# Source order for TensorE, ScalarE and VectorE in a gated mix of linear attention and a squared-ReLU MLP

## The chip, the cores and the metric

The kernel runs on one core of a Trainium2 chip. A core has engines that run side by side, each with an instruction queue of its own: TensorE (PE in the profile, matmuls into PSUM banks; PEld are its weight loads), VectorE (DVE), ScalarE (ACT), GpSimd (POOL) and SyncE (SP, which here only starts DMAs). They wait for each other by semaphores. The metric is the device time of one execution in microseconds (us).

## What is computed

For x of 2048 tokens by 448, with 16 heads of 28 and a hidden width of 1792:

```python
qkv = (x @ wqkv) ...            # q, k, v: 16 heads of 28
phi = lambda t: jnp.where(t > 0, t + 1, jnp.exp(t)) + 1e-6
pq, pk = phi(q), phi(k)
kv = jnp.einsum("bhsd,bhse->bhde", pk, v)
z = jnp.einsum("bhsd->bhd", pk)
num = jnp.einsum("bhqd,bhde->bhqe", pq, kv)
den = jnp.einsum("bhqd,bhd->bhq", pq, z)[..., None] + 1e-6
a = (num / den) ... @ wo
h = jnp.einsum("bsd,df->bsf", x, w1) + b1
r = jnp.where(h > zero, h, zero)
b = jnp.einsum("bsf,fd->bsd", r * r, w2) + b2
g = _sigmoid((x * gate_w).sum(-1, keepdims=True))
return g * a + (1 - g) * b
```

Everything is float32.

## The kernel before

Every float32 operand of a matmul is split into a high part (rounded to the matmul's own type, the name ends in h) and a low part (the rest, the name ends in l), and a product is made as high by high, high by low and low by high. The high part is a copy with a conversion, mostly on ACT (`split_hi`, line 58) and for the hidden values on DVE (line 62); the low part is a subtraction on DVE, for `nl` on POOL (`split_lo`, line 65).

The tokens are four blocks of 512, each of four tiles of 128. The hidden width is 14 chunks f of 128. `up(b, f)` makes the hidden chunk in `h_ps` (line 214: 11 matmuls of 512 columns, since the last of four chunks c of the 448 inputs needs two terms only), `hidden` takes ReLU and square on ACT (lines 222, 223, tile `hr`) and splits on DVE (`hh`, `hl`), and `down(b, f)` adds the chunk to the four output tiles `o_ps` (line 245: 12 matmuls of 448 columns). An up is always one chunk ahead of its down.

Pass 1 goes over blocks 0 to 3 with f 0 to 6. It also makes, tile by tile, the keys (`k_ps`, 11 matmuls of 448 columns, `phi` into `r`, split into `ph` and `pl`), the gate's logits, and per block the gram of keys and tokens (`g_ps`, 11 or 8 matmuls for each of four c, out of the `ph`, `pl` and the split tokens `nh`, `nl` of all four tiles). Then key sums and the product with v are made. Pass 2 goes over blocks 3, 0, 1, 2 with f 7 to 13, each with queries (`q_ps`, c = 3 first; `swap` brings the last query chunk's partitions into order with eight DMAs `qr<-qv`, `join` adds both), the sum `ds` of queries times key sums, its split `dh`, `dl`, the matmul `d_ps` that spreads it over a head, `rec` (1e-6 added, four reciprocals), the scaled queries (`qh`, `ql`) and, tile by tile, `attention` (`a_ps`, 11 matmuls, then `u` on ACT and `part` on DVE). In the first of these blocks the matrix `m_s` is made out of `wo` and the gram: four m products, each split and then moved by five DMAs on POOL's queue. `finish` adds the gated parts and stores a tile.

PSUM has eight banks: four for `o_ps` (pool `acc_p`), two for `h_ps` (`mm_p`), two for everything else (`ms_p`, taken in turn by the scheduler's count). SBUF buffers for short-lived tiles come from 15 slots.

The source gives the steps in a rough order, with the parts that follow a matmul put off by `run_todo`. The order on every engine is decided by a scheduler: it interleaves the matmuls of one step with those of another and picks, on ACT and DVE, what its own plan has ready first. One place is tied by hand, with `tc.issue_after`, which keeps `d_ps` behind the last down (line 454).

At the start, 18 matmuls on zeros keep PE at work (line 164) while x and w1 come in by chunks c, w1 before x, the first x in two halves; the first four hidden chunks are made together, chunk c by chunk c (lines 501 to 512).

Of the kernel before, what the change touches and what calls it, by code (L numbers as in the profile page):

```python
# [30 lines left out]
def gated_mix_kernel(ctx: ExitStack, tc: tile.TileContext, xt, xn, wk, wq, wv, wo, w1a, w1b, w2, b1, b2, gw, hmask,  # L31
# [125 lines left out]

    warm = keep.tile([P, 400], mybir.dt.bfloat16, name="warm")[:, :256]  # L160
    dve.memset(warm, 0.0)
    warm_ps = acc_p.tile([P, 512], F, name="warm_ps", tag="acc")
    for _ in range(18):
        pe.matmul(warm_ps[:, :256], warm[:, :P], warm, start=True, stop=True)
# [39 lines left out]
    def up_chunk(ps, b, f, c):  # L204
# [8 lines left out]
        for n, (a, m) in enumerate(terms):  # L213
            pe.matmul(ps, a, m, start=(c == 0 and n == 0), stop=(c == 3 and n == 1))  # L214
# [546 lines left out]
```

## Time and profile before

| | |
|---|---|
| time, median of 3 runs (lowest, highest) | 441.72 us (441.72, 441.75) |
| the profiled execution, and its span | 441.68 us, 439.9 us |
| granted TensorE clock, mean | 0.998 |
| busy: PE, DVE, ACT, POOL | 431.6, 281.4, 172.2, 63.0 us |
| first matmul of the computation, start of the last | 5.28 us, 435.57 us |

A row of the timeline gives the start in us from the span's start, the duration, the engine, the line, the operation with output and inputs by the program's names, the shape and how many instructions are grouped; in brackets the idle time just before it and what ended it. A row of the waits gives the waiting engine with its output, what it waited for, the total, the number of times and the longest. A row of the issues of DMAs ends with the count, the size and the median us from issue to landing.

### The profile page before, as it was taken

The numbers are of one execution on the slowest core, as the hardware profiler recorded it, in microseconds if no ns is written. First come the engines' busy times: TensorE is split into PE (matmuls) and PEld (weight loads), VectorE is DVE, ScalarE is ACT, GpSimd is POOL, SyncE is SP. The second block draws the span as 40 slices with busy tenths as digits, with TensorE's granted clock in tenths as the row PEclk, the third lists the DMA queues.
The fourth block names the chain that finished last, engine by engine and source line by source line (L and its number), as shares of the span: only waits on it lengthen the run. The fifth ranks groups of instructions, "written<-read, shape, count | busy, mean of one in ns | idle before, by whom it ended". The sixth has DMA issues, their size and how long they took to land.

```text
span 439.9 us, 5510 instructions
## 1 busy us (share of the span) xinstructions
PE 431.6 (98%) x2054; PEld 380.5 (86%) x2054; DVE 281.4 (64%) x470; ACT 172.2 (39%) x300; POOL 63.0 (14%) x76
## 2 busy tenths in 40 slices
PE   8999899999999999999999989999999999999996
PEld 6898798899898889898988868889888898888895
DVE  5969538662689428792466678788455984549423
ACT  5955235331346113542344335345332453234321
POOL 0144124210244005420002420000000000000000
PEclk9999999999999999999999999999999999999999
DMA  8852302021031210332146311040100501002002
GB/s 268 224 155 58 99 0 66 28 66 47 24 115 34 67 45 5 107 102 82 54 125 148 73 38 24 1 154 26 25 0 0 182 0 25 0 1 85 0 1 83
DMA packets 18459, 29.00 MB, mean 66 GB/s; under 512 B 2896, under 2 KB 12928, under 8 KB 18432
## 3 DMA queue, kind: packets, MB, share of 16 engines
q1 hardware_dynamic: 17216, 27.04, 20.3%
q0 software_dynamic: 1216, 1.61, 1.9%
q8 instruction: 16, 0.26, 0.3%
q14 instruction: 11, 0.09, 0.1%
HBM read 22.31 MB, written 3.67 MB: 59 GB/s over the span
## 4 chain that ended last, share of the span: by engine, by line
PE 90%; DVE 4%; ACT 1%; issue 1%; DMA 1%; SPq 1%; DVEq 0%; ACTq 0%
PE o_ps L245 29%; PE h_ps L214 28%; PE q_ps L77 8%; PE a_ps L77 8%; PE g_ps L77 8%; PE k_ps L77 7%; DMA xr<-in_xt 1%; PE kv_ps L372 1%; SPq L51 1%; PE m_ps L77 1%; DVE w L65 1%; DVE wk_s L65 0%; ACT hr L222 0%; DVE r L266 0%; PE d_ps L77 0%
## 5 line engine op out<-in xcount | busy, mean ns | idle before, releaser
L214 PE MATMUL h_ps<-xh,w 128*128 128x512 f32 x392 | 126.5, 391 | 0.5 <-ACT xh L58 0.4
L245 PE MATMUL o_ps<-w,hh 128*128 128x448 f32 x448 | 125.5, 363 | 0.4 <-DVE hh L62 0.4
L245 PEld LDWEIGHTS o_ps<-w,hh 128*128 128x128 f32 x448 | 83.9, 188 | 9.7 <-DVE hh L62 1.0
L214 PE MATMUL h_ps<-xl,w 128*128 128x512 f32 x224 | 87.6, 391 | 0.0
L214 PEld LDWEIGHTS h_ps<-xh,w 128*128 128x128 f32 x392 | 73.6, 188 | 15.2 <-ACT xh L58 0.7
L245 PE MATMUL o_ps<-w,hl 128*128 128x448 f32 x224 | 79.9, 364 | 0.0
L222 ACT ACTIVATE hr<-h_ps,b_s 128x512 f32<-128x512 f32 (+1 forms) x57 | 38.4, 675 | 97.3 <-PE h_ps L214 90.2
L62 DVE CAST hh<-hr 128x512 fp32r<-128x512 f32 (+1 forms) x57 | 26.1, 458 | 39.1 <-ACT hr L223 38.9
L214 PEld LDWEIGHTS h_ps<-xl,w 128*128 128x128 f32 x224 | 42.1, 188 | 8.2 <-DVE xl L65 0.5
L245 PEld LDWEIGHTS o_ps<-w,hl 128*128 128x128 f32 x224 | 42.1, 188 | 2.9 <-DVE hl L65 0.2
L65 DVE TENSOR_TENSOR hl<-hr,hh 128x512 fp32r<-128x512 f32 (+1 forms) x57 | 41.2, 722 | 1.9
L223 ACT ACTIVATE hr<-hr 128x512 f32<-128x512 f32 (+1 forms) x57 | 35.3, 622 | 1.3
L77 PE MATMUL k_ps<-wk_s,xh 128*128 128x448 f32 x112 | 33.0, 362 | 0.0
L77 PE MATMUL q_ps<-xh,wq_s 128*128 128x512 f32 x100 | 33.0, 390 | 0.0
L65 POOL TENSOR_TENSOR nl<-xnr,nh 128x384 fp32r<-128x384 f32 x16 | 18.7, 1166 | 95.2 <-ACT nh L58 95.2
L77 PE MATMUL a_ps<-m_s,qh 128*128 128x448 f32 x112 | 32.2, 362 | 0.0
L289 POOL TENSOR_TENSOR ksum<-ksum,r 128x448 f32<-128x448 f32 x15 | 22.8, 1517 | 46.7 <-DVE r L266 41.3
L490 DVE SCALAR_TENSOR_TENSOR part<-part,gate,u 128x448 f32<-128x448 f32 x16 | 10.9, 683 | 24.9 <-ACT u L489 24.9
L489 ACT ACTIVATE u<-a_ps,gate 128x448 f32<-128x448 f32 x16 | 10.1, 634 | 37.2 <-PE a_ps L77 37.2
L77 PE MATMUL g_ps<-ph,nh 128*128 128x448 f32 x64 | 23.2, 363 | 0.7 <-ACT ph L58 0.7
L77 PE MATMUL g_ps<-pl,nh 128*128 128x448 f32 x64 | 23.3, 364 | 0.5 <-DVE pl L65 0.5
L77 PE MATMUL q_ps<-xl,wq_s 128*128 128x512 f32 x60 | 23.4, 390 | 0.0
(105 smaller groups left out, 562.2 us busy)
## 6 DMA issues: line engine op xcount, KB each, us to landing
xr<-in_xt SPq DMA_DIRECT2D x27, 256.0 KB, 2.8
xnr<-in_xn SPq DMA_DIRECT2D x16, 224.0 KB, 2.6
out<-out SPq DMA_DIRECT2D x16, 224.0 KB, 2.0
w2r<-in_w SPq DMA_DIRECT2D x14, 224.0 KB, 2.7
w1r<-in_w1a SPq DMA_DIRECT2D x8, 256.0 KB, 2.7
w1r<-in_w1b SPq DMA_DIRECT2D x8, 192.0 KB, 2.9
m_s<-m POOLq DMA_DIRECT2D x12, 112.0 KB, 2.6
wqr<-in_wq SPq DMA_DIRECT2D x4, 256.0 KB, 3.1
```

Source lines behind the costliest of these rows:

```text
L51: sp.dma_start(out=dst, in_=src)
L62: eng.tensor_copy(hi, src)
L65: eng.tensor_tensor(lo, src, f32(hi), op=ALU.subtract)
L77: pe.matmul(out_ps, a, b, start=(i == 0), stop=(i == n - 1))
L214: pe.matmul(ps, a, m, start=(c == 0 and n == 0), stop=(c == 3 and n == 1))
L222: act.activation(r[:, c], ps[:, c], AF.Relu, bias=b1_s[:, f:f + 1])
L223: act.activation(r[:, c], r[:, c], AF.Square)
L245: last = pe.matmul(o_ps[i][:, :D], a, m, start=(f % NH == 0 and n == 0), stop=(f % NH == NH - 1 and n == 2))
L289: pool.tensor_tensor(ksum, ksum, p, op=ALU.add)
L372: pe.matmul(kv_ps[:JE, js], wv_s[c][:, js], gsum[c][:, js], start=(c == 0), stop=(c == 3))
L489: act.activation(u, ps[:, :D], AF.Copy, scale=gate[:, 0, t:t + 1])
L490: dve.scalar_tensor_tensor(part[t], part[t], gate[:, 1, t:t + 1], u, op0=ALU.mult, op1=ALU.add)
```

## The change

The change has three parts. First, PE, ACT and DVE take their instructions in the order of the source (`tc.manual_schedule`); SP and POOL stay with the scheduler. The source is rewritten to be that order: `run_todo` stands ahead of an up or behind it as the place needs, with `join` steps last; the keys' work is cut into `first` and `rest`; `split_den`, `denominators`, `scaled`, `attention`, the splits of wo and of the kv product, and the m products have places of their own; and the end of the last block takes its last attention behind up 13 and the two last chunks' downs in the order 12 for three tiles, then 13, with the fourth tile last. Second, the start: x is loaded before w1, the first w1 chunk in two halves, the twelve matmuls of the first chunk go term by term over the four hidden chunks, 15 warm-up matmuls stand where 18 did (on zeros that lie in `part[0]`), the second group of w1 is loaded behind wk, and the keys of tile 0 stand ahead of the first down, with their PSUM banks out of `acc_p` and `mm_p`. Third, buffers and small steps: the two other PSUM banks are taken by name in turn (`bank`), the m products use `mm_p`, 1e-6 is added by one ACT copy from PSUM into `rec` in place of two DVE additions of 256 columns, half of the swap's DMAs are issued by POOL, the split kv and wo tiles lie in the late pool, and some weights' tiles change their padding.

The core of the diff:

```diff
+    ms_p = ctx.enter_context(tc.tile_pool(name="ms_p", bufs=1, space=PSUM))
+    turn = [0]
+
+    def bank(name):
+        turn[0] ^= 1
+        return ms_p.tile([P, 512], F, name=name, tag=f"ms{turn[0]}")
 
...
+    ctx.enter_context(tc.manual_schedule(engines={pe.engine, act.engine, dve.engine}))
+
+
+    part = [keep.tile([P, D], F, name=f"part{t}") for t in range(NT)]
+    warm = part[0].bitcast(mybir.dt.bfloat16)[:, :256]
     dve.memset(warm, 0.0)
     warm_ps = acc_p.tile([P, 512], F, name="warm_ps", tag="acc")
-    for _ in range(18):
+    for _ in range(15):
         pe.matmul(warm_ps[:, :256], warm[:, :P], warm, start=True, stop=True)
...
     for c in range(4):
-        load_w1(0, 0, c)
+        load_x(0, c)
         if c == 0:
-            load_x(0, c, 0, TB // 2)
-            load_x(0, c, TB // 2, TB)
-        else:
-            load_x(0, c)
+            load_w1(0, 0, c, 0, TB // 2)
+            load_w1(0, 0, c, TB // 2, TB)
+        else:
+            load_w1(0, 0, c)
...
-        def after():
+        def first():
             phi(ps[:, :D], e, r, p)
+
+        def rest():
+            nh = tmp.tile([P, 512], R, name=f"nh{t}", tag="nh", bufs=4)
+            nl = tmp.tile([P, 384], R, name=f"nl{t}", tag="nl", bufs=4)
+            raw = xn_raw.pop(t)
+            split_hi(act, nh[:, :D], raw)
+            split_lo(pool, nl, raw[:, :384], nh[:, :384])
+            split_lo(pool, nh[:, D:], raw[:, 384:], nh[:, 384:D])
+            dve.scalar_tensor_tensor(e, raw, 1.0, gw_s, op0=ALU.mult, op1=ALU.mult, accum_out=logit[:, t:t + 1])
             split_hi(act, ph, p)
             split_lo(dve, pl, p, ph)
             if t == 0:
                 pool.tensor_copy(ksum, p)
             else:
                 pool.tensor_tensor(ksum, ksum, p, op=ALU.add)
-            nh = tmp.tile([P, 512], R, name=f"nh{t}", tag="nh", bufs=4)
-            nl = tmp.tile([P, 384], R, name=f"nl{t}", tag="nl", bufs=4)
-            raw = xn_raw[t]
-            split_hi(act, nh[:, :D], raw)
-            split_lo(pool, nl, raw[:, :384], nh[:, :384])
-            split_lo(pool, nh[:, D:], raw[:, 384:], nh[:, 384:D])
             pend[t] = (ph, pl, nh, nl)
-            return [logits]
...
             act.copy(v, ps)
-            for p in range(0, P, 16):
-                load(r[p:p + 16], v[p ^ 16:(p ^ 16) + 16])
+            for p in range(0, P, 32):
+                load(r[p:p + 16], v[p + 16:p + 32])
+                pool.dma_start(out=r[p + 16:p + 32], in_=v[p:p + 16])
             return [join]
...
-        ps = ms_p.tile([P, 512], F, name=f"d_ps{b}", tag="ms")
-        with tc.issue_after(last.ins):
-            products(ps, [(hm, den.pop((b, "h"))), (hm, den.pop((b, "l")))])
+    def split_den(b):
+        den[b, "h"], den[b, "l"] = slot([P, TB], R, f"dh{b}"), slot([P, TB], R, f"dl{b}")
+        total = den.pop((b, "s"))
+        split_hi(act, den[b, "h"], total)
+        split_lo(dve, den[b, "l"], total, den[b, "h"])
+
+    def denominators(b):
+        ps = bank(f"d_ps{b}")
+        products(ps, [(hm, den.pop((b, "h"))), (hm, den.pop((b, "l")))])
         den[b, "r"] = rec = slot([P, TB], F, f"rec{b}")
 
+        act.activation(rec, ps, AF.Copy, bias=1e-6)
+
         def part_(i):
-            cs = slice(i * 256, (i + 1) * 256)
-            dve.tensor_scalar_add(rec[:, cs], ps[:, cs], 1e-6)
             for j in range(2 * i, 2 * i + 2):
                 dve.reciprocal(rec[:, j * P:(j + 1) * P], rec[:, j * P:(j + 1) * P])
         return [lambda: part_(0), lambda: part_(1)]
...
     def run_todo():
-        now, todo[:] = list(todo), []
+        now, todo[:] = sorted(todo, key=lambda step: step.__name__ == "join"), []
...
+    first = [mm_p.tile([P, 512], F, name=f"h_ps0_{f}", tag="mm") if f < 2 else bank(f"h_ps0_{f}") for f in range(4)]
     for c in range(4):
         if c == 0:
-            split_x(0, 0, 0, TB // 2)
-            split_w1(0, 0, 0, hi_eng=dve)
-            split_x(0, 0, TB // 2, TB)
-        else:
+            xs[0] = new_x(0)
+            w, raw = new_w1(0, 0), w1_raw.pop((0, 0, 0))
+            xh, xl = [x[:, 0] for x in xs[0]]
+            split_hi(act, xh, x_raw[0, 0])
+            split_hi(dve, w[:, 0, :TB // 2], raw[:, :TB // 2])
+            split_lo(dve, xl, x_raw[0, 0], xh)
+            split_hi(dve, w[:, 0, TB // 2:], raw[:, TB // 2:])
+            split_lo(dve, w[:, 4], raw, w[:, 0])
+        else:
+            split_x(0, c)
             split_w1(0, 0, c)
-            split_x(0, c)
-        for f in range(4):
-            up_chunk(first[f], 0, f, c)
-    hidden(first[0], 0, 0, 2)
-    hidden(first[1], 0, 1)
+        if c == 0:
+            for n in range(3):
+                for f in range(4):
+                    up_chunk(first[f], 0, f, c, n)
+        else:
+            for f in range(4):
+                up_chunk(first[f], 0, f, c)
     split_w2(0)
     split_w2(1)
-    for f in range(2, 4):
-        hidden(first[f], 0, f)
-
-    wk_s = keep.tile([P, 7 * D + 48], R, name="wk_s", tag="wkm", bufs=1)
-    wk_s = wk_s[:, :7 * D].rearrange("p (c n) -> p c n", c=7)
-
-    load_xn(0)
+    wk_s = keep.tile([P, 7, D], R, name="wk_s", tag="wkm", bufs=1)
+    for c in range(4):
+        split_w(wk_s, c, wk_raw[c], act, dve)
+    load(gw_s, gw.partition_broadcast(P))
+    load(b2_s, b2.partition_broadcast(P))
+    hidden(first[0], 0, 0)
+    hidden(first[1], 0, 1)
+    k_first, k_rest = keys(0)
+    down(0, 0)
+    k_first()
+    for c in range(4):
+        split_w1(0, 1, c)
     load_w2(2)
     load_w2(3)
-    for c in range(4):
-        split_w(wk_s, c, wk_raw[c], act, dve)
-    down(0, 0)
...
     load_x(1, 3)
     split_x(1, 1)
     split_w2(6)
-    todo += gram(0, 0)
     split_x(1, 2)
     down(0, 5)
-    run_todo()
-    todo += gram(0, 1)
+    todo += gram(0, 0)
     split_x(1, 3)
 
...
                 if b == 1:
-                    todo += gram(0, 2)
-                    run_todo()
-                    todo += gram(0, 3)
-                    run_todo()
+                    for c in range(1, 4):
+                        todo += gram(0, c)
+                        run_todo()
             else:
...
         for f in range(NF - NH, NF):
             fl = f - NH
             run_todo()
+            if fl == (0 if n else 4) and n != 1:
+                split_den(b)
             up(b, f)
...
+                split_x(then, 2 * fl - 2)
+                split_x(then, 2 * fl - 1)
             if fl:
                 if n + 1 < NB or f + 1 < NF:
-                    last = down(b, f - 1)
+                    down(b, f - 1)
             elif n == 0:
                 down(b, NH - 1)
                 half_done(b)
             else:
-                last = down(order[n - 1], NF - 1)
+                down(order[n - 1], NF - 1)
                 for i in range(4):
+                    if n == 1:
+                        attention(order[0], i)
                     finish(order[n - 1], i)
             if n == 0:
                 if fl < 4:
...
-                        attention(b, i)
+                    m_product(2)
+                for c in ((0,), (1, 2, 3))[fl - 5] if fl >= 5 else ():
+                    scaled(b, c)
+                if fl >= 4:
+                    for c in ((3,), (0,), (1, 2))[fl - 4]:
+                        todo += queries(then, c)
+                if fl == 4:
+                    todo += denominators(b)
+                elif 2 <= fl < 6:
+                    m_product(fl - 2)
             else:
                 if fl == 0:
-                    todo += denominators(b, last)
-                if fl == 1:
-                    for c in range(4):
-                        scaled(b, c)
-                if 2 <= fl < 6:
-                    attention(b, fl - 2)
-            if then is not None:
-                if fl < 2:
-                    load_x(then, 2 * fl)
-                    load_x(then, 2 * fl + 1)
-                if 1 <= fl < 3:
-                    split_x(then, 2 * fl - 2)
-                    split_x(then, 2 * fl - 1)
-                if n and 3 <= fl:
+                    todo += denominators(b)
+                if 2 <= fl < 4:
+                    scaled(b, 2 * fl - 4)
+                    scaled(b, 2 * fl - 3)
+                for i in (((0,), (1,), (2, 3)) if then is not None else ((0, 1), (2,), (3,)))[fl - 4] if fl >= 4 else ():
+                    attention(b, i)
+                if then is not None and 3 <= fl:
                     todo += queries(then, (3, 0, 1, 2)[fl - 3])
-                if n == 0 and fl in (5, 6):
-                    for c in ((3, 0), (1, 2))[fl - 5]:
-                        todo += queries(then, c)
+    last = order[-1]
+    down(last, NF - 2, range(3))
     for i in range(4):
-        for f in (NF - 2, NF - 1):
-            down(order[-1], f, [i])
-        finish(order[-1], i)
```

Where the rows move, on PE at the start of the program: `h_ps0_2` is block 0's hidden chunk 2, `o_ps0_0_1` the output of block 0, chunk 0, tile 1, `k_ps0` the keys of tile 0. Before:

```order
L214 MATMUL h_ps0_2_164<-xl0_167,w1_00_170 128x512
L214 MATMUL h_ps0_3_165<-xh0_166,w1_00_170 128x512
L214 MATMUL h_ps0_3_165<-xl0_167,w1_00_170 128x512
L245 MATMUL o_ps0_0_0_285<-w2_0_250,hh0_0_233 128x448 x2
L245 MATMUL o_ps0_0_1_289<-w2_0_250,hh0_0_233 128x448
L245 MATMUL o_ps0_0_0_285<-w2_0_250,hl0_0_234 128x448
L245 MATMUL o_ps0_0_1_289<-w2_0_250,hh0_0_233 128x448
```

With the change:

```order
L232 MATMUL h_ps0_2_170<-xl0_173,w1_00_174 128x512
L232 MATMUL h_ps0_3_171<-xh0_172,w1_00_174 128x512
L232 MATMUL h_ps0_3_171<-xl0_173,w1_00_174 128x512
L84 MATMUL k_ps0_268<-wk_s_243,xh0_172 128x448 x2
L84 MATMUL k_ps0_268<-wk_s_243,xl0_173 128x448
L84 MATMUL k_ps0_268<-wk_s_243,xh0_172 128x448 x2
L84 MATMUL k_ps0_268<-wk_s_243,xl0_173 128x448
L84 MATMUL k_ps0_268<-wk_s_243,xh0_172 128x448 x2
L84 MATMUL k_ps0_268<-wk_s_243,xl0_173 128x448
L84 MATMUL k_ps0_268<-wk_s_243,xh0_172 128x448
L84 MATMUL k_ps0_268<-wk_s_243,xl0_173 128x448
L261 MATMUL o_ps0_0_0_286<-w2_0_237,hh0_0_257 128x448 x2
```

The eleven matmuls of the keys of tile 0 came between the matmuls of the second down; now they stand between the last of the first ups and the first down.

On PE at the denominators of the first pass-2 block, which is block 3 (`h_ps3_12` is its up 12, `m_ps2` the m product 2, `q_ps0_3` the queries of the following block 0). Before:

```order
L214 MATMUL h_ps3_12_2378<-xh3_1326,w1_11_2125 128x512 x2
L214 MATMUL h_ps3_12_2378<-xl3_1327,w1_11_2125 128x512
L214 MATMUL h_ps3_12_2378<-xh3_1326,w1_11_2125 128x512 x2
L214 MATMUL h_ps3_12_2378<-xl3_1327,w1_11_2125 128x512
L77 MATMUL d_ps3_2368<-dh3_2333,hm_136 128x512
L214 MATMUL h_ps3_13_2469<-xh3_1326,w1_11_2125 128x512
L77 MATMUL d_ps3_2368<-dl3_2334,hm_136 128x512
L214 MATMUL h_ps3_13_2469<-xl3_1327,w1_11_2125 128x512
```

With the change:

```order
L84 MATMUL m_ps2_2337<-woh2_2247,kv_h_2046 128x448
L84 MATMUL m_ps2_2337<-wol2_2248,kv_h_2046 128x448
L84 MATMUL m_ps2_2337<-woh2_2247,kv_l_2047 128x448
L84 MATMUL q_ps0_3_2349<-xh0_2180,wq_s_167 128x512
L84 MATMUL q_ps0_3_2349<-xl0_2181,wq_s_167 128x512
L84 MATMUL q_ps0_3_2349<-xh0_2180,wq_s_167 128x512
L84 MATMUL q_ps0_3_2349<-xl0_2181,wq_s_167 128x512
L84 MATMUL q_ps0_3_2349<-xh0_2180,wq_s_167 128x512
L84 MATMUL q_ps0_3_2349<-xl0_2181,wq_s_167 128x512
L84 MATMUL q_ps0_3_2349<-xh0_2180,wq_s_167 128x512
L84 MATMUL d_ps3_2360<-dh3_2298,hm_158 128x512
L84 MATMUL d_ps3_2360<-dl3_2299,hm_158 128x512
```

The two matmuls of `d_ps` stood behind up 12, each beside one of up 13; now they stand ahead of up 12, behind an m product and the first queries of the next block.

On DVE at the start of the third block of pass 2, which is block 1 (`out0` is tile 0 of the block before it). Before:

```order
L62 CAST hh1_7_3045<-hr1_7_3044 128x512
L65 TENSOR_TENSOR hl1_7_3046<-hr1_7_3044,hh1_7_3045 128x512
L256 SCALAR_TENSOR_TENSOR out0_3063<-o_ps0_7_0_2681,gate_119,part0_139 128x448
L256 SCALAR_TENSOR_TENSOR out1_3066<-o_ps0_7_1_2685,gate_119,part1_140 128x448
L256 SCALAR_TENSOR_TENSOR out2_3069<-o_ps0_7_2_2689,gate_119,part2_141 128x448
L256 SCALAR_TENSOR_TENSOR out3_3072<-o_ps0_7_3_2693,gate_119,part3_142 128x448
L460 TENSOR_SCALAR rec1_3078<-d_ps1_3075 128x256 x2
L462 RECIPROCAL rec1_3078<-rec1_3078 128x128 x4
L62 CAST hh1_8_3102<-hr1_8_3101 128x512
L470 TENSOR_TENSOR qe1_0_2903<-rec1_3078,qe1_0_2903 128x512
L65 TENSOR_TENSOR hl1_8_3103<-hr1_8_3101,hh1_8_3102 128x512
```

With the change:

```order
L69 CAST hh1_7_3038<-hr1_7_3035 128x512
L72 TENSOR_TENSOR hl1_7_3039<-hr1_7_3035,hh1_7_3038 128x512
L271 SCALAR_TENSOR_TENSOR out0_3058<-o_ps0_7_0_2682,gate_133,part0_75 128x448
L271 SCALAR_TENSOR_TENSOR out1_3061<-o_ps0_7_1_2686,gate_133,part1_76 128x448
L271 SCALAR_TENSOR_TENSOR out2_3064<-o_ps0_7_2_2690,gate_133,part2_77 128x448
L271 SCALAR_TENSOR_TENSOR out3_3067<-o_ps0_7_3_2694,gate_133,part3_78 128x448
L482 RECIPROCAL rec1_3073<-rec1_3073 128x128 x4
L69 CAST hh1_8_3094<-hr1_8_3091 128x512
L72 TENSOR_TENSOR hl1_8_3095<-hr1_8_3091,hh1_8_3094 128x512
```

The two additions into `rec` are gone from DVE, and a scaled query that stood between `hh1_8` and `hl1_8` is put off.

More of the change, by code (lines that the diff above doesn't have):

```diff
@@ L194, in gated_mix_kernel @@
     ksum = keep.tile([P, D], F, name="ksum")
-    part = [keep.tile([P, D], F, name=f"part{t}") for t in range(NT)]
     phase1 = ExitStack()
@@ L244, in down @@
             for n, (a, m) in enumerate(terms):
-                last = pe.matmul(o_ps[i][:, :D], a, m, start=(f % NH == 0 and n == 0),
-                                 stop=(f % NH == NH - 1 and n == 2))
-        return last
+                pe.matmul(o_ps[i][:, :D], a, m, start=(f % NH == 0 and n == 0),
+                          stop=(f % NH == NH - 1 and n == 2))
     def half_done(b):
@@ L269, in keys @@
         b, i = divmod(t, 4)
-        ps = ms_p.tile([P, 512], F, name=f"k_ps{t}", tag="ms")
+        if t < 2:
+            ps = (acc_p, mm_p)[t].tile([P, 512], F, name=f"k_ps{t}", tag=("acc", "mm")[t])
+        else:
+            ps = bank(f"k_ps{t}")
         products(ps[:, :D], [term for c in range(4)
@@ L319, in gram @@
         return [after]
-    wq_s = keep.tile([P, 7, TB], R, name="wq_s")
+    wq_s = keep.tile([P, 8 + 7 * TB], R, name="wq_s")[:, 8:]
+    wq_s = wq_s.rearrange("p (c n) -> p c n", c=7)
     wq_raw = {}
@@ L348, in key_sums @@
         pool.tensor_copy(zk[:, 3, :, :16], ks[:, :, 96:])
-        z_ps = ms_p.tile([P, 512], F, name="z_ps", tag="ms")
+        z_ps = bank("z_ps")
         for c in range(4):
@@ L367, in kv_product @@
     def kv_product():
-        kv_ps = ms_p.tile([P, 512], F, name="kv_ps", tag="ms")
+        kv_ps = bank("kv_ps")
         for j in range(NJ):
@@ L380, in kv_product, with late_tile @@
             dve.tensor_copy(t[:, :, JE:], f32(t[:, :, 96:JE]))
+    def late_tile(shape, name, dt=R):
+        return late.tile(shape, dt, name=name, tag="q", bufs=NLATE)
     wo_raw, wo_s = {}, {}
@@ L479, in attention @@
         cols = slice(i * P, (i + 1) * P)
-        ps = ms_p.tile([P, 512], F, name=f"a_ps{t}", tag="ms")
+        ps = bank(f"a_ps{t}")
         terms = []
@@ L524, in gated_mix_kernel @@
     load_w2(2)
     load_w2(3)
[L526 to L528 removed]
+    load_xn(0)
     load_xn(1)
[L530 to L538 removed]
+    hidden(first[2], 0, 2)
+    hidden(first[3], 0, 3)
+    down(0, 1)
+    k_rest()
+    todo += keys(1)
+    split_w2(2)
@@ L539, in gated_mix_kernel @@
     split_w2(3)
-    for c in range(4):
-        split_w1(0, 1, c)
     load_xn(2)
@@ L686, in gated_mix_kernel @@
+                for c in ((0,), (1, 2, 3))[fl - 5] if fl >= 5 else ():
[7 more added lines that the diff above has]
+                    m_product(fl - 2)
             else:
                 if fl == 0:
-                    todo += denominators(b, last)
-                if fl == 1:
-                    for c in range(4):
-                        scaled(b, c)
@@ L709, in gated_mix_kernel @@
-        finish(order[-1], i)
+        if i == 3:
+            down(last, NF - 2, [i])
+        down(last, NF - 1, [i])
+        finish(last, i)
 def kernel(**inputs):
```

171 lines of the change are left out of this document (81 added, 90 removed).

## The prediction

> **What bounds the kernel now.** I read the page first (busy shares and the chain that ended last), then the waits of PE, then PE's timeline around each wait. The profiled execution took 441.68 us, of which the span is 439.9; the median of the runs shown is 441.72, so both scales agree within 0.04 us.
>
> ```profile
> PE 431.6 (98%) x2054; PEld 380.5 (86%) x2054; DVE 281.4 (64%) x470; ACT 172.2 (39%) x300; POOL 63.0 (14%) x76
> PE 90%; DVE 4%; ACT 1%; issue 1%; DMA 1%; SPq 1%; DVEq 0%; ACTq 0%
> 282.00:336.00 54.00, 54.00 (x255) 47.39 (x254) 36.20 (x59) 20.02 (x33) 0.00 (x0) 1.00 0.13 42
> ```
>
> PE is 98% busy and carries 90% of the chain. From 282 to 336 (pass 2, one whole block; columns: length, PE, PEld, DVE, ACT, POOL, granted clock, DMA share, GB/s) it has no idle time at all, at clock 1.00. The change keeps every matmul of the computation, so it can only win what PE loses by waiting. PE's waits:
>
> ```profile
> PE d_ps L77 <- ACT dh L58: 1.3, 1, 1.3
> PE g_ps L77 <- ACT ph L58: 0.7, 1, 0.7
> PE g_ps L77 <- DVE pl L65: 0.5, 1, 0.5
> ```
>
> The timeline shows what each costs. Matmuls overlap, so I count from start to start. Undisturbed, a matmul of 512 columns takes 0.226 (eight start from 254.28 to 256.09 below, 1.81 us) and one of 448 columns 0.20 (47.98 to 48.18). What a stretch takes beyond that is the stall, which is larger than the idle time in brackets. Ahead of the first down:
>
> ```profile
> 15.37 0.39 PE L214 MATMUL h_ps<-xl,w 128*128 128x512 f32 x1
> 16.11 0.88 PE L245 MATMUL o_ps<-w,hh 128*128 128x448 f32 x3 [0.35 <-DVE hh L62]
> 16.82 0.36 PE L245 MATMUL o_ps<-w,hl 128*128 128x448 f32 x1
> ```
>
> 1.45 for one of 512 and three of 448 (0.83): 0.62. In block 0's gram:
>
> ```profile
> 46.39 0.57 PE L245 MATMUL o_ps<-w,hh 128*128 128x448 f32 x2
> 47.67 0.47 PE L77 MATMUL g_ps<-ph,nh 128*128 128x448 f32 x1 [0.71 <-ACT ph L58]
> 47.98 0.37 PE L245 MATMUL o_ps<-w,hl 128*128 128x448 f32 x1
> 48.18 0.57 PE L245 MATMUL o_ps<-w,hh 128*128 128x448 f32 x2
> 49.22 0.47 PE L77 MATMUL g_ps<-pl,nh 128*128 128x448 f32 x1 [0.46 <-DVE pl L65]
> 49.53 0.36 PE L77 MATMUL g_ps<-ph,nl 128*128 128x448 f32 x1
> ```
>
> 1.59 for three (0.60): 0.99; then 1.35 for three: 0.75. At the denominators of the first pass-2 block, with the first and the last link of their chain on ACT and DVE:
>
> ```profile
> 254.28 0.62 PE L214 MATMUL h_ps<-xh,w 128*128 128x512 f32 x2
> ...
> 256.09 0.39 PE L214 MATMUL h_ps<-xl,w 128*128 128x512 f32 x1
> 257.81 0.50 PE L77 MATMUL d_ps<-dh,hm 128*128 128x512 f32 x1 [1.32 <-ACT dh L58]
> 258.38 0.50 PE L214 MATMUL h_ps<-xh,w 128*128 128x512 f32 x1
> ```
>
> ```profile
> 254.25 0.60 ACT L264 ACTIVATE qe<-q_ps 128x512 f32<-128x512 f32 x1 [6.36 <-PE q_ps L77]
> ```
>
> ```profile
> 257.79 0.69 DVE L65 TENSOR_TENSOR dl<-ds,dh 128x512 fp32r<-128x512 f32 x1 [0.69 <-ACT dh L58]
> ```
>
> 2.29 for two of 512: 1.84. And in the tail, where hidden 13 is late for its down:
>
> ```profile
> 432.47 1.13 PE L245 MATMUL o_ps<-w,hh 128*128 128x448 f32 x4
> 433.45 0.47 PE L245 MATMUL o_ps<-w,hl 128*128 128x448 f32 x1
> 433.76 0.37 PE L245 MATMUL o_ps<-w,hh 128*128 128x448 f32 x1
> ```
>
> 1.29 for five (1.00): 0.29. Together 4.49 us.
>
> **The change part by part.** *Start.* The rows that fix when the first chunk's operands are there, on PE, DVE and ACT:
>
> ```profile
> 1.06 3.84 PE L164 MATMUL warm_ps<-warm 128*128 128x256 bf16 x18 [1.06 <-DVE warm L161]
> 5.28 0.74 PE L214 MATMUL h_ps<-xh,w 128*128 128x512 f32 x2 [0.38 <-ACT xh L58]
> ```
>
> ```profile
> 3.43 0.43 DVE L62 CAST w<-w1r 128x512 fp32r<-128x512 f32 x1 [2.17 <-DMA w1r<-in_w1a]
> 3.89 0.69 DVE L65 TENSOR_TENSOR w<-w1r,w 128x512 fp32r<-128x512 f32 x1
> ```
>
> ```profile
> 3.73 0.42 ACT L58 ACTIVATE xh<-xr 128x256 fp32r<-128x256 f32 x1 [1.70 <-DMA xr<-in_xt]
> 4.81 0.42 ACT L58 ACTIVATE xh<-xr 128x256 fp32r<-128x256 f32 x1 [0.67 <-DMA xr<-in_xt]
> 6.39 0.63 ACT L58 ACTIVATE w<-w1r 128x512 fp32r<-128x512 f32 x1 [1.16 <-DMA w1r<-in_w1a]
> 7.03 0.63 ACT L58 ACTIVATE xh<-xr 128x512 fp32r<-128x512 f32 x1
> ```
>
> The loads swap places in SP's order with equal bytes: 256 KB land at 3.4, then halves at 3.7 and 4.8. The whole xh is then ready at 3.4+0.63 = 4.1, half of w by 4.1; fifteen warm-ups of 3.84/18 = 0.213 end at 4.25. Two of the twelve matmuls run then (before: the first at 5.28); the other two hidden chunks wait for w's second half until about 5.15, and the low part of w (0.69 behind that cast) is ready by 5.85, when the n-outer order first asks for it after eight matmuls at 6.5. The chunk ends near 7.4. Chunk 1 now gets x at 6.4 and w at 7.03, ready at 7.7, its low part at 8.4: stalls of 0.28 and 0.26. From 8.4 on, 32 less 2 matmuls remain, and no later operand is late (the loads behind are the same bytes in swapped pairs): 8.4+30*0.226 = 15.2, against 15.6 before: **-0.38**. Three warm-ups fewer are 0.64 us less early work; if PE reached its full rate that much later, at most half, 0.32, is lost, and the wait for w's second half hides it.
>
> *Keys(0) ahead of the first down.* Eleven matmuls (2.2 us) now stand where PE waited for hh.
>
> ```profile
> 13.38 2.35 DVE L65 TENSOR_TENSOR wk_s<-wkr,wk_s 128x448 fp32r<-128x448 f32 x4
> ```
>
> ```profile
> 20.71 2.10 DVE L65 TENSOR_TENSOR w<-w2r,w 128x448 fp32r<-128x448 f32 x2
> ```
>
> The wk splits end at 15.7, hh follows, the down starts at 17.4: cover over 1 us. **-0.62**. What is late next: the fourth tile of that down needs the bank of k_ps0, free when ACT's exp and DVE's max have read it, two operations of some 0.6 behind the keys' end at 17.4, and it is asked for nine matmuls (1.8) after that end: some 0.4 of slack. Then down(0,2) near 27 needs w2's low part, which DVE now takes behind the logits and pl of tile 0. The pair took 2.10 here, 1.05 each, while POOL worked; the same operation took 2.35/4 = 0.59 with POOL idle. By the one or the other it is ready between 26.3 and 27.8 and asked for at 26.9: nothing to 0.9. I take **+0.1**, nearest to the undisturbed row.
>
> *Grams.* gram(0,0) moves behind down(0,5), so the two waits at 47.67 and 49.22 lose their cause: pl of tile 3 comes some 2 us ahead. **-1.74**. The cover is 12 matmuls of down and what stands before; with it gone the 1.74 come back.
>
> *Denominators of the first pass-2 block.* The chain from exp to dl took 254.25 to 258.48, 4.2 us. In the new order PE has up 11, down 10, an m product and seven of q_ps 3 between the queries and d_ps: 18*0.226+15*0.20 = 7.1 us. With an m split (0.6) in DVE's line ahead of it the chain is 2 us early. **-1.84**. Late next: DVE's queue behind it. After the fourth m product DVE has hh, hl 13, three scaled products with their splits and the next queries in source order, and the first queries' banks are asked for within 0.2 us of being read; the third attention's bank waits for ACT's copy of u behind a dh. I put **+0.3** for both, from nothing (all hidden) to 1.0 (one split round of ACT and DVE, 0.63+0.69, less 0.3 of slack).
>
> *Pass-2 block ends.* In the three other blocks DVE does four outs, four reciprocals and only then hh 8:
>
> ```profile
> 293.09 3.38 DVE L462 RECIPROCAL rec<-rec 128x128 f32<-128x128 f32 x4
> 296.38 0.36 DVE L62 CAST hh<-hr 128x512 fp32r<-128x512 f32 x1
> ```
>
> This was so before too, and the rec additions leave DVE (ACT does one instead), so hh comes no later against PE unless the added ACT step waits behind relu and square; slack 0.2 to 0.6. **+0.2** in all, from nothing to 0.75 in each of two blocks.
>
> *Tail.* The last attention behind up 13 covers hidden 13: **-0.29**. PSUM banks by name, the kv and wo tiles and the offsets of weights add no instruction; each at nothing, since PE's pitch stands by the matmul's columns.
>
> *Swap by two queues.* Half its DMAs go from SP to POOL, behind the m tiles' DMAs there:
>
> ```profile
> 249.19 1.60 POOL L406 DMA_DIRECT2D m_s<-m  x3 [0.51 <-DVE m L65]
> ```
>
> ```profile
> m_s<-m POOLq DMA_DIRECT2D x12, 112.0 KB, 2.6
> qr<-qv SPq DMA_DIRECT2D x32, 32.0 KB, 1.9
> ```
>
> Four POOL issues take 4*0.53 = 2.1, landing by 2.6: 4.7 and a copy of 0.6, 5.3 us after q_ps 3. PE has two d_ps, eleven up, twelve down and eleven queries between (24*0.226+12*0.2 = 7.8), so the join, which stands behind those queries in DVE's order, has 2.5 to spare. Nothing.
>
> The Trainium skill, "SBUF — State Buffer", section "SBUF: two separate sides" and its part "A bandwidth-pool intuition that's wrong", speaks against this edit: a DMA issued by GpSimd has its descriptors written by GpSimd, which is locked out while VectorE runs a two-port mode; it gives about 620 ns alone and 3100 ns beside such a copy. Worked out from that page, an estimate, four swaps would land 2.5 us later, just what is to spare, so the sum would stay. The m tiles' rows here do not show it: three issues take 1.60 with DVE at work.
>
> Sum: -0.38-0.62-1.74-1.84-0.29 = -4.87; +0.1+0.3+0.2 = +0.6; **-4.27**. 441.68-4.27 = **437.4 us**.
>
> **The rivals.** *Order gives part back.* The three soft places cost their upper ends (0.9+1.0+1.5 = 3.4): -4.87+3.4 = -1.47, **440.2**. For it: three engines now wait in line, so one late operand holds all behind it, where the scheduler put other work there. Against: DVE is at 64%.
>
> *The waits only move.* The gaps close where they are named but each comes back one step on, since hh, dh and ph are made by the same chains: only the start and the tail remain: -0.38-0.29 = -0.67, **441.0**. Against: PE is idle at five places only, and the new order puts 2 us of other matmuls before four of them.
>
> *Slower: the join.* If POOL's four DMAs land over 2.5 us later than I count, DVE stands at the join, and behind it hh, so PE stalls, four times. Each further us costs 4 us; from about 3.6 us late (4*1.1 against 4.27) it is slower than before; at 4, 4*1.5-4.27 = +1.7: **443.4**. For it: m's five DMAs ahead of one swap on the queue. Against: only one of the four swaps meets them, and before's POOL issues keep 0.53.
>
> **How the numbers follow.** Forecast 0.63 (436.5, with all soft places free: 441.68-4.87 = 436.8 and 0.3 below for small gaps at the start, to 438.6); order gives back 0.23 (438.6 to 440.8); waits only move 0.08; join 0.04; faster still 0.02. The range is 436.5 to 440.6. Within 0.2% (about what a measurement of this kernel can tell from no change) means 440.8 to 442.6: same 0.08, slower 0.04, faster 0.88.
>
> **What would show it.** PE's timeline without waits near 16, 47, 49 and 257, the first real matmul near 4.3 with short waits to 5.2, 7.7 and 8.4, the keys directly behind the first ups, no gap between o_ps at the end. Against me: o_ps waiting for w2 near 27, a_ps for ACT's u near 270, o_ps for hh 8 after each block, DVE idle before qv on a DMA, or a PE pitch other than 0.226 and 0.20.

## The result and the profile after

The changed kernel takes 437.79 us (median of 5 runs, 437.56 to 438.17) against 441.75 us before (5 runs on the same chip, 441.72 to 442.13). The ratio is 0.9909 with a 95% interval of 0.9894 to 0.9923. The forecast was 437.4 in a range of 436.5 to 440.6. The profiled execution took 437.56 us with a span of 435.8; its page, engines and the chain that ended last:

```profile
PE 430.4 (99%) x2051; PEld 380.7 (87%) x2051; DVE 286.5 (66%) x460; ACT 174.0 (40%) x301; POOL 70.7 (16%) x92
PE 93%; DVE 4%; ACT 1%; DMA 1%; issue 0%; DVEq 0%; ACTq 0%
```

PE is three matmuls shorter (the warm-ups), its share of the chain is 93% instead of 90%. What PE still waits for, by the view of waits (the longer idle times of PE; short stalls don't stand in it):

```profile
PE warm_ps L180 <- DVE part L177: 1.1, 1, 1.1
PE a_ps L84 <- ACT u L509: 0.2, 1, 0.2
```

The waits at d_ps, g_ps and o_ps are gone. The timeline of PE at the five places of before, and at two new ones:

```profile
14.81 0.39 PE L232 MATMUL h_ps<-xl,w 128*128 128x512 f32 x1
15.03 0.37 PE L84 MATMUL k_ps<-wk_s,xh 128*128 128x448 f32 x1
```

```profile
26.55 0.39 PE L232 MATMUL h_ps<-xl,w 128*128 128x512 f32 x1
26.78 0.93 PE L261 MATMUL o_ps<-w,hh 128*128 128x448 f32 x2
27.55 0.36 PE L261 MATMUL o_ps<-w,hl 128*128 128x448 f32 x1
```

```profile
45.95 0.36 PE L261 MATMUL o_ps<-w,hl 128*128 128x448 f32 x1
46.15 0.36 PE L84 MATMUL g_ps<-ph,nh 128*128 128x448 f32 x1
```

```profile
251.91 0.40 PE L84 MATMUL q_ps<-xh,wq_s 128*128 128x512 f32 x1
252.15 0.39 PE L84 MATMUL d_ps<-dh,hm 128*128 128x512 f32 x1
252.38 0.40 PE L84 MATMUL d_ps<-dl,hm 128*128 128x512 f32 x1
```

```profile
279.80 0.36 PE L84 MATMUL a_ps<-m_s,ql 128*128 128x448 f32 x1
280.38 0.67 PE L84 MATMUL a_ps<-m_s,qh 128*128 128x448 f32 x2 [0.21 <-ACT u L509]
280.89 0.36 PE L84 MATMUL a_ps<-m_s,ql 128*128 128x448 f32 x1
```

The first ups end at 15.03 (15.60 before) and the keys follow at once. The gram and d_ps start at PE's undisturbed pace (0.20 and 0.24 after the matmul ahead of them). Two stalls are new: 26.78 to 27.55 is 0.77 for two matmuls of 0.20, 0.37 too long, at the low part of w2; 279.80 to 280.89 is 1.09 for three, 0.49 too long, at the bank of the third attention.

### The profile page after: what moved, and what is told of

Its sections match the earlier page's. It is cut to its first block, busy times and chain, and to the rows that moved or that the text cites. A ratio compares the mean times of both kernels' runs of the same rounds, so it can differ in the third digit from the quotient of the medians.

```text
span 435.8 us, 5547 instructions
## 1 busy us (share of the span) xinstructions
PE 430.4 (99%) x2051; PEld 380.7 (87%) x2051; DVE 286.5 (66%) x460; ACT 174.0 (40%) x301; POOL 70.7 (16%) x92
## 4 chain that ended last, share of the span: by engine, by line
PE 93%; DVE 4%; ACT 1%; DMA 1%; issue 0%; DVEq 0%; ACTq 0%
PE h_ps L232 31%; PE o_ps L261 30%; PE g_ps L84 8%; PE k_ps L84 8%; PE q_ps L84 7%; PE a_ps L84 7%; PE warm_ps L180 1%; PE kv_ps L389 1%; DVE qe L281 1%; DMA w2r<-in_w 1%; PE m_ps L84 1%; DVE ds L452 1%; DVE ql L72 0%; PE d_ps L84 0%; DVE qe L490 0%; DVE qr L280 0%
## 5 line engine op out<-in xcount | busy, mean ns | idle before, releaser
L261 PE MATMUL o_ps<-w,hl 128*128 128x448 f32 x224 | 81.3, 363 | 0.0
L236 ACT ACTIVATE hr<-h_ps,b_s 128x512 f32<-128x512 f32 x56 | 38.0, 679 | 77.6 <-PE h_ps L232 72.3
L69 DVE CAST hh<-hr 128x512 fp32r<-128x512 f32 x56 | 24.3, 434 | 48.0 <-ACT hr L237 47.9
L72 DVE TENSOR_TENSOR hl<-hr,hh 128x512 fp32r<-128x512 f32 x56 | 38.9, 694 | 3.1
L237 ACT ACTIVATE hr<-hr 128x512 f32<-128x512 f32 x56 | 35.4, 632 | 1.8
L72 POOL TENSOR_TENSOR nl<-xnr,nh 128x384 fp32r<-128x384 f32 x16 | 16.4, 1023 | 120.6 <-ACT nh L65 120.6
L459 POOL DMA_DIRECT2D qr<-qv x16 | 8.1, 515 | 122.8 <-ACT qv L456 122.8
L280 DVE TENSOR_SCALAR r<-k_ps 128x448 f32<-128x448 f32 x16 | 10.0, 623 | 21.9 <-ACT e L279 21.9
L72 DVE TENSOR_TENSOR pl<-r,ph 128x448 fp32r<-128x448 f32 x16 | 23.4, 1463 | 0.0
L84 PE MATMUL a_ps<-m_s,ql 128*128 128x448 f32 x64 | 23.2, 363 | 0.0
```

What stands on the lines that cost most here:

```text
L69: eng.tensor_copy(hi, src)
L72: eng.tensor_tensor(lo, src, f32(hi), op=ALU.subtract)
L84: pe.matmul(out_ps, a, b, start=(i == 0), stop=(i == n - 1))
L236: act.activation(r, ps, AF.Relu, bias=b1_s[:, f:f + 1])
L237: act.activation(r, r, AF.Square)
L261: pe.matmul(o_ps[i][:, :D], a, m, start=(f % NH == 0 and n == 0), stop=(f % NH == NH - 1 and n == 2))
```

## The experiments

Eleven kernels, each run beside the kernel before on the same chip. They vary the changed kernel unless the text says otherwise. Times are medians; a few tenths of a us are read from the traces, since the intervals are about 0.1 to 0.23% wide to each side.

### The place of the first gram

```diff
+    todo += gram(0, 0)
     split_x(1, 2)
     down(0, 5)
-    todo += gram(0, 0)
```

> gram(0,0) goes back ahead of the down of chunk 5, where it stood before the change; everything else as in the changed kernel (437.8 us). Theory A, the step of the prediction (the wait at the first gram went because the gram moved behind twelve matmuls of down): PE waits at g_ps for ph and pl again, about 1.7 us, 439.5. Theory B (it went because the keys of tile 3 are taken up by ACT and DVE some 5 us earlier, ahead of up 6 and its hidden values): the gram's last terms are asked for at 45.6, ph is ready at 42.2 and pl at 43.8, so no wait, 437.8 within 0.3.

Measured: 437.98 us, ratio 0.9909 (0.9887 to 0.9932), and no wait at g_ps. Theory A is refuted as it stands: the twelve matmuls of down are not needed as a cover. Next, the same with the keys' steps behind the up:

```diff
-    run_todo()
     up(0, 6)
+    run_todo()
     down(0, 4)
```

> As e1, and the steps that follow the keys of tile 3 stand behind up 6 and its hidden values on ACT and DVE (as the scheduler had them) instead of ahead of up 6. Theory B: ph comes near 46 and pl near 48, the gram's terms of tile 3 are asked for at 45.6 to 45.8: PE waits about 2 us in all at g_ps, 439.5 to 440. Theory A: no more than in e1.

Measured: 441.06 us, ratio 0.9982 (0.9967 to 0.9998); the view of waits:

```profile
PE g_ps L84 <- DVE pl L72: 1.1, 1, 1.1
...
PE g_ps L84 <- ACT ph L65: 0.5, 1, 0.5
```

Both waits of before are back, pl's larger than it was: from 45.78 to 48.57 three matmuls take 2.79 instead of 0.60, 2.19 us of stall, as expected. The median is above the 439.5 to 440 expected. Five of its ten executions, at a granted clock of 0.998 to 1.00 (the profiled one, 440.18, among them), took 440.08 to 440.60; the other five, at 0.994 to 0.996, took 441.51 to 442.27. More on that at the end.

What was not run is the gram behind the down with the keys' steps late, the move that the prediction named. An estimate from this trace: ph is done at 46.62 and pl at 48.20, and twelve matmuls of 0.20 later the gram would ask for them at 48.38 and 48.58. So that move by itself might have closed the waits too.

Then the same move alone in the kernel before, under its scheduler:

```diff
-    up(0, 6)
     run_todo()
+    up(0, 6)
```

(and so for ups 4 and 5)

> The kernel before, under its scheduler, with one part of the change alone: in block 0 the steps that follow the keys of a tile stand ahead of ups 4, 5 and 6 instead of behind them. If their place in the source is what brought ph and pl late to the first gram, the waits at g_ps go (1.74 us): 440.0. If the scheduler's own plan set it whatever the source says, or other parts of the change are needed with it, 441.7.

Measured: 440.08 us, ratio 0.9965 (0.9955 to 0.9974); g_ps no longer stands in the view of waits, d_ps still does (1.3). What moved is seen on ACT, in the kernel before and in this one, by the exp of tile 3's keys:

```profile
44.20 0.53 ACT L264 ACTIVATE e<-k_ps 128x448 f32<-128x448 f32 x1
```

```profile
40.04 0.55 ACT L264 ACTIVATE e<-k_ps 128x448 f32<-128x448 f32 x1 [1.48 <-PE k_ps L77]
```

On PE the keys give way to the next up at 39.69 in the first and 39.85 in the second. Before, exp stood behind ReLU and square of up 6 in ACT's line and started at 44.20; with the steps ahead of the up it starts at 40.04, and ph, which the gram asks for, starts at 42.80 instead of 47.04. With the gram where it was, that place in the source is what the 1.74 us were.

### The cover of the denominators

```diff
+            if n == 0 and fl == 4:
+                todo += denominators(b)
             if fl:
                 ...
-                if fl == 4:
-                    todo += denominators(b)
```

> In the first block of pass 2, d_ps stands directly behind up 11, ahead of the down of chunk 10, an m product and the first queries of the next block (5 us of other matmuls), with the same steps on ACT and DVE. If these matmuls are what hides the chain from the queries to dl (ready at 249.3 for dh and 250.0 for dl, in the changed kernel's trace; asked for at 252.15), d_ps is asked for near 247.5 and PE waits about 2 us: 439.6 to 440. If the chain had become shorter in itself and needs no cover, no wait: 437.8.

Measured: 440.42 us, ratio 0.997 (0.9958 to 0.9982). PE's timeline:

```profile
248.03 0.39 PE L232 MATMUL h_ps<-xl,w 128*128 128x512 f32 x1
250.11 0.50 PE L84 MATMUL d_ps<-dh,hm 128*128 128x512 f32 x1 [1.69 <-ACT dh L65]
250.83 0.50 PE L84 MATMUL d_ps<-dl,hm 128*128 128x512 f32 x1 [0.23 <-DVE dl L72]
251.17 0.37 PE L261 MATMUL o_ps<-w,hh 128*128 128x448 f32 x1
```

248.03 to 251.17 is 3.14 for three matmuls of 0.226: 2.46 us of stall, a little more than the 2 expected. The chain from exp to dl is as long as ever (246.38 to 250.78 here, 4.4 us, as in the changed kernel; 4.2 before); the cover hides it.

Why was it late before? In the kernel before, the queries c = 2 ran on PE from 251.54 only. The two banks that queries share were then held by m products, two at a time, and on ACT the copies of the second and the third product waited for the m tile's DMAs, as its timeline before shows:

```profile
241.24 0.54 ACT L58 ACTIVATE m<-m_ps 128x448 fp32r<-128x448 f32 x1 [0.41 <-DMA m_s<-m]
...
247.35 0.55 ACT L58 ACTIVATE m<-m_ps 128x448 fp32r<-128x448 f32 x1 [1.06 <-DMA m_s<-m]
```

DVE's subtraction behind it, the last step that reads this bank, ends at 248.9; the queries came 2.6 us later, behind a down, so the bank is not the whole of the delay. To try this, the kernel before with two places of the change:

```diff
-        ps = ms_p.tile([P, 512], F, name=f"m_ps{j}", tag="ms")
+        ps = mm_p.tile([P, 512], F, name=f"m_ps{j}", tag="mm")
...
-                if fl in (1, 2):
-                    for j in range(2 * fl - 2, 2 * fl):
-                        split_wo(j)
-                        todo += m_product(j)
+                if 1 <= fl < 5:
+                    split_wo(fl - 1)
+                    todo += m_product(fl - 1)
...
```

(with the keys' steps of the experiment above)

> The kernel before, under its scheduler, with two places of the change alone: the keys' steps ahead of the ups in block 0 (as in e5, 440.1) and the m products one per hidden chunk, their results in the ups' PSUM banks instead of the banks of the queries. Theory: in the kernel before, the queries c = 1 and 2 waited for banks that m products held until the m tile's DMAs had landed, and so dh came late to d_ps; with this the last queries come two hidden chunks earlier and the wait at d_ps (1.84) goes: 438.2. Rival: the wait at d_ps is the scheduler's order or the missing cover behind it, and stays: 440.1, or the ups wait for the banks that m products now take, 440 to 442.

Measured: 440.63 us (440.05 to 441.51), ratio 0.9972 (0.9959 to 0.9985), so nothing gained over 440.08. The wait at d_ps is gone from the view of waits, as the theory says, and another stands in its stead, a down that has only its own up ahead of it:

```profile
246.67 0.77 PE L245 MATMUL o_ps<-w,hl 128*128 128x448 f32 x3
248.78 0.88 PE L245 MATMUL o_ps<-w,hh 128*128 128x448 f32 x3 [0.74 <-DVE hh L62]
```

246.67 to 248.78 is 2.11 for three: 1.5 us. The profiled execution (441.06) also lost 1.9 us at its start, to which I come below. The cause of the late queries is supported by this, not more: bank and number of products were changed together, and the wait moved.

### Who sets the order

```diff
-    ctx.enter_context(tc.manual_schedule(engines={pe.engine, act.engine, dve.engine}))
```

> The changed source with the order of PE, ACT and DVE left to the scheduler again. If the source's order on the engines is what closes the waits, most of them come back and only the start and the smaller steps are left: 440 to 441. If the rewritten source (its steps' places, the early loads, the banks) does it and the scheduler follows it, 437.8 to 438.5.

Measured: 437.72 us, ratio 0.9903 (0.988 to 0.9926): the same as the changed kernel. Its waits:

```profile
PE warm_ps L179 <- DVE part L176: 1.1, 1, 1.1
PE h_ps L231 <- DVE xl L72: 0.2, 1, 0.2
```

The scheduler interleaves again and has neither of the two new stalls. So the gain comes from the rewritten source, its steps' places, start and buffers; that the engines take it word for word adds nothing that the clock can tell. In the profiled execution the first ups end at 15.88, 0.85 us later than in the changed kernel's, about as much as the two stalls took; whether that is scatter of the start or the scheduler's order is not shown.

### Keys ahead of the first down, and what an order in line can cost

```diff
-    k_first, k_rest = keys(0)
     down(0, 0)
+    k_first, k_rest = keys(0)
     k_first()
```

(and the bank of k_ps0 comes out of `mm_p`)

> The changed kernel with the first down ahead of the keys of tile 0 (their PSUM bank then comes from the ups' two). If the eleven matmuls of the keys are what covers the splits of wk and of the first hidden chunk, PE waits at the first o_ps for hh (ready near 16.2, asked for near 15.2) and for hl (16.9): 1.2 to 1.6 us there, some 0.6 to 1 more than before the change, because the first chunk is no longer split in halves; 439.0 to 439.4. If the earlier start alone closed that wait, nothing: 437.8.

Measured: 443.28 us (441.82 to 444.68), ratio 1.0041 (1.0026 to 1.0056), well above the 439.0 to 439.4 expected. The profiled execution, at a granted clock of 1.00, took 441.82, as long as the kernel before; the four others, at 0.992 to 0.996, took 443.11 to 444.68. PE's timeline (span 440.0, 4.2 more than the changed kernel's):

```profile
15.10 0.39 PE L232 MATMUL h_ps<-xl,w 128*128 128x512 f32 x1
16.15 0.68 PE L261 MATMUL o_ps<-w,hh 128*128 128x448 f32 x2 [0.66 <-DVE hh L69]
16.88 0.47 PE L261 MATMUL o_ps<-w,hl 128*128 128x448 f32 x1
17.19 0.36 PE L261 MATMUL o_ps<-w,hh 128*128 128x448 f32 x1
...
28.31 0.37 PE L261 MATMUL o_ps<-w,hh 128*128 128x448 f32 x1
31.41 0.47 PE L261 MATMUL o_ps<-w,hh 128*128 128x448 f32 x1 [2.73 <-DVE w L72]
```

The first down waits 2.09-0.83 = 1.26, as expected. The 2.9 us at 28.31 were not: DVE's first step for the keys now comes at 21.97 (18.02 in the changed kernel), 3.95 later, and all that stands behind it in DVE's line is late with it. w2's low part, which has nothing to do with the keys, comes at 30.62 instead of 25.75, 4.87 later, as pl just ahead of it also took 1.41 instead of 0.61. The change of bank is not the cause: on PE the keys run without a wait.

```profile
21.97 0.62 DVE L280 TENSOR_SCALAR r<-k_ps 128x448 f32<-128x448 f32 x1 [4.02 <-ACT e L279]
30.62 1.27 DVE L72 TENSOR_TENSOR w<-w2r,w 128x448 fp32r<-128x448 f32 x2
```

### The two remaining waits

```diff
+    split_w2(2)
     k_rest()
     todo += keys(1)
-    split_w2(2)
...
-            if fl == 0 and n == 1:
-                split_den(b)
...
                         attention(order[0], i)
+                        if i == 1:
+                            split_den(b)
```

> The changed kernel with its two remaining waits taken away by order: w2's second split ahead of the logits and pl of tile 0 (the wait of 0.37 at the second o_ps near 27), and in the second block of pass 2 dh and dl behind the first two copies of u (the wait of 0.48 at the third a_ps near 280). If the waits are made by what stands ahead of them in the lines of DVE and ACT, both go and nothing else comes: 437.8-0.85 = 436.9. If each is only passed on, 437.5 to 437.8 with waits at hl or pl and at dh.

Measured: 437.26 us (436.85 to 439.08), ratio 0.9905 (0.9883 to 0.9927), span 435.1 against 435.8. By the view of waits PE waits for nothing but the first zeros; in the timeline both stalls are gone, with no gap near 27 and near 280. By the clock this can't be told from the changed kernel.

### Start, tail and the addition on ACT

The start as before (18 warm-ups; the first chunk hidden chunk by hidden chunk):

```diff
-        load_x(0, c)
+        load_w1(0, 0, c)
         if c == 0:
-            load_w1(0, 0, c, 0, TB // 2)
-            load_w1(0, 0, c, TB // 2, TB)
...
```

> The changed kernel with the start as before: w1 ahead of x, x's first chunk in halves, 18 warm-ups, the first chunk's matmuls hidden chunk by hidden chunk. By the prediction the keys then begin 0.38 later than with the new start: 438.2; the keys' first matmul at 15.6 in the trace (15.0 to 15.9 in the five traces of the new start, by when x's second chunk lands). If the new start is worth nothing beyond the scatter of the loads, 437.8.

Measured: 438.35 us (438.19 to 438.6), ratio 0.9923 (0.9908 to 0.9937). The keys' first matmul stands at 16.04, beyond the 14.95 to 15.75 that the eight profiled executions with the new start in this order have for the end of the first ups. The direction agrees; 0.6 us is within what a measurement can hardly tell.

The last attention ahead of up 13:

```diff
-                for i in (((0,), (1,), (2, 3)) if then is not None else ((0, 1), (2,), (3,)))[fl - 4] if fl >= 4 else ():
+                for i in (((0,), (1,), (2, 3)) if then is not None else ((0, 1), (2, 3), ()))[fl - 4] if fl >= 4 else ():
```

> The changed kernel with the last attention ahead of up 13 as before. By the prediction's step the wait for hidden 13 in the tail returns: 0.29 in the trace's last 5 us (438.1), as three short gaps between o_ps. If the tail gained by the new order of the last downs, none.

Measured: 438.84 us (438.3 to 439.07), ratio 0.9928 (0.9913 to 0.9943). The gaps come back larger:

```profile
428.41 0.37 PE L261 MATMUL o_ps<-w,hl 128*128 128x448 f32 x1
428.87 0.67 PE L261 MATMUL o_ps<-w,hh 128*128 128x448 f32 x2
429.66 0.47 PE L261 MATMUL o_ps<-w,hl 128*128 128x448 f32 x1
429.98 0.36 PE L261 MATMUL o_ps<-w,hh 128*128 128x448 f32 x1
```

428.41 to 429.98 is 1.57 for four of 0.20: 0.77 us. In the kernel before, the scheduler had interleaved the last downs otherwise, with one more matmul ahead of the first that waits and one more between the two waits, and it was 0.29.

1e-6 added on DVE in two pieces, as before:

```diff
-        act.activation(rec, ps, AF.Copy, bias=1e-6)
...
+            cs = slice(i * 256, (i + 1) * 256)
+            dve.tensor_scalar_add(rec[:, cs], ps[:, cs], 1e-6)
```

> The changed kernel with 1e-6 added by DVE in two pieces, as before, instead of by one ACT copy. In the changed kernel's trace DVE has done hl 8 at 345.6 and PE asks for it near 345.9 (hh 8 0.6 ahead of its use); 0.66 more in DVE's line there makes PE wait 0.3 to 0.5 at o_ps for hl 8 in each of two or three blocks: 438.5 to 439.0. If the slack is larger than it looks, nothing: 437.8.

Measured: 439.14 us (439.09 to 439.65), ratio 0.9936 (0.992 to 0.9953). In the third block of pass 2 (and alike in the fourth, at 399.4):

```profile
345.89 0.39 PE L232 MATMUL h_ps<-xl,w 128*128 128x512 f32 x1
346.42 0.67 PE L261 MATMUL o_ps<-w,hh 128*128 128x448 f32 x2
347.15 0.47 PE L261 MATMUL o_ps<-w,hl 128*128 128x448 f32 x1
347.46 0.36 PE L261 MATMUL o_ps<-w,hh 128*128 128x448 f32 x1
```

345.89 to 347.46 is 1.57 for four (0.83): 0.74 us in each of two blocks, more than the 0.3 to 0.5 expected. DVE's hh 8 and hl 8 in the changed kernel, then hh 8 here:

```profile
344.52 0.36 DVE L69 CAST hh<-hr 128x512 fp32r<-128x512 f32 x1
344.92 0.69 DVE L72 TENSOR_TENSOR hl<-hr,hh 128x512 fp32r<-128x512 f32 x1
```

```profile
346.01 0.36 DVE L69 CAST hh<-hr 128x512 fp32r<-128x512 f32 x1
```

In the changed kernel PE asks for them at 345.55 and 345.95, so the slack is 0.67 at hh and 0.34 at hl. From the step behind the four outs to hh DVE takes 4.21 here (341.80 to 346.01) against 3.29 there (341.23 to 344.52): the additions cost 0.92, not 0.66, and PE waits at both operands.

## Why the prediction held, step by step

| step | predicted | in the profiled execution |
|---|---|---|
| start | -0.38 | -0.57 (15.60 to 15.03) |
| keys ahead of the first down | -0.62 | -0.62, no gap |
| down at w2's low part | +0.1 | +0.37 |
| first gram | -1.74 | -1.74, no gap |
| d_ps | -1.84 | -1.84, no gap |
| queue behind it, third attention | +0.3 | +0.49 |
| ends of pass-2 blocks | +0.2 | 0 |
| tail | -0.29 | -0.29, no gap |
| sum | -4.27 | -4.20; the executions differ by 441.68-437.56 = 4.12 |

That the sum came out so close is in part luck: four terms are off by -0.19, +0.27, +0.19 and -0.20, which cancel to +0.07.

**Right with its reason:** keys(0) (undone, 1.26 us come back), d_ps (its cover undone, 2.46), the tail (undone, 0.77). The d_ps chain was said to be 2 us early: dl was done at 250.0 and asked for at 252.38. The third attention waits for ACT's u behind a dh, as said; with dh behind u the wait is gone.

**Supported, its size open:** the start. The first ups end at 14.95 to 15.75 in eight profiled executions with the new start in this order, and at 15.60, 15.90 and 16.04 in three with the old one (a fourth, at half pace, is told of below); the 0.57 of the table compares one with one.

**Right in size, its reason not the one at work:** the first gram. The prediction gave the 1.74 to "gram(0,0) moves behind down(0,5), so the two waits ... lose their cause" and said of the down's matmuls "with it gone the 1.74 come back". That failed: with the gram back in its old place there is no wait. The place of the keys' steps ahead of the up is enough by itself, shown in both directions with the gram early, and the prediction left it out. That the gram's move alone would have done it too is likely by the estimate above, but not shown. As the number hangs on neither, its being right says nothing for the reason.

**Without weight:** "three engines now wait in line", counted for the rival in which order gives part back. The scheduler on the same source gives 437.72, so the line as a whole neither cost nor gained what the clock can tell.

**Right in its reason, too dear:** the ends of pass-2 blocks, +0.2 against 0. That the additions leave DVE was named as what keeps hh in time, and it is needed there: without it 0.74 are lost twice.

**Sizes off:** w2's low part lay 0.27 above the value taken, inside its bounds (nothing to 0.9), the third attention 0.19 above (0.49 against +0.3). For w2, DVE beside POOL was the right side of the bound: the pair took 2.09 from 25.75 on, and its first, for which the down waits, 1.43. The join did not matter: POOL's DMAs `qr<-qv` landed 1.9 us after issue, SP's 2.2. The starvation that the Trainium skill ("SBUF — State Buffer", "SBUF: two separate sides") describes for GpSimd's DMAs beside VectorE is not seen here; whether VectorE ran a two-port mode beside them, no trace shows.

The rival "order gives part back" exists as a mechanism: one step late in the line cost 2.9 us at an unrelated place in the experiment with the first down ahead of the keys. In the changed kernel it took the 0.37 and 0.49 and no more, since that step was not late.

## What to carry to other kernels

A wait is cured by the step that makes its operand, not only by moving the step that asks for it: look first at where exp, split and sum stand in the lines of the helping engines. When two edits could each close a wait, undo each alone before one of them is given the credit. Where engines take the source's order, each step moved late holds back what stands behind it, related or not, so undo one place at a time and read the trace far behind it. And before giving a hand-written order the credit, let the scheduler try the rewritten source.
